# One-operand maxima and sums, a turned ring of banks, and two loads moved in SP's queue

## The chip, the cores and the metric

The kernel runs on one core of one Trainium2 chip. The time is that of one execution on the device, in microseconds, and the median over the runs counts. One further execution was profiled; its trace and its page are what the profile below is read from.

Engine names: PE is TensorE (PEld its weight loads), DVE is VectorE, ACT is ScalarE, POOL is GpSimd, SP is SyncE, which only issues DMAs here.

## What is computed

Two attentions over the same shapes, side by side in the output: sequence 2048, width 576, 32 heads of 18. A is a dilated sliding window of 8 keys, B is full attention.

```python
def _A_ref(x, wqkv, wo):
...
    W, dil = 8, 2
...
    q, k, v = qkv[0], qkv[1], qkv[2]
    off = jnp.arange(W) * dil
    idx = pos[:, None] - off[None, :]
...
    kg = k[:, :, idx_c, :].reshape(B, H, S, W, Dh)
    vg = v[:, :, idx_c, :].reshape(B, H, S, W, Dh)
    logits = jnp.einsum("bhsd,bhswd->bhsw", q, kg) * scale
    logits = jnp.where(mask[None, None, :, :], logits, -1e9)
    attn = _softmax(logits, axis=-1)
    o = jnp.einsum("bhsw,bhswd->bhsd", attn, vg)
    return (lambda x, *d: x.transpose(*d))(o, 0, 2, 1, 3).reshape(B, S, D) @ wo

def _B_ref(x, wqkv, wo):
...
    scores = jnp.einsum("bhqd,bhkd->bhqk", q, k) * scale
    p = _softmax(scores, axis=-1)
    o = jnp.einsum("bhqk,bhkd->bhqd", p, v)
    return (lambda x, *d: x.transpose(*d))(o, 0, 2, 1, 3).reshape(B, S, D) @ wo

return jnp.concatenate([a, b], axis=-1)
```

## The kernel before

**Two parts in time.** The first part projects: B's and A's queries, keys and values by matmuls over the width, in split precision (each operand as a high and a low half). The second part, which the change is about, is one loop over 512 **steps**. Step s works on one key tile kt = s % 16 of 128 keys, one block b of 512 queries (four blocks) and one group g of four heads (eight groups): s = 64 g + 16 b + kt.

**One step of B.** TensorE makes four score tiles (`score`, L271; one bank of PSUM each, 128 keys x 512 queries), ScalarE turns each into exponentials (L279), and one step later four matmuls (L744, eight rows in the profile) multiply them with the values into the accumulating bank `po`. The values carry a column of ones, so `po` also holds the softmax's denominators. In the same step TensorE makes raw scores again for the maxima of a block that comes later (L160), and VectorE reduces three banks of them to maxima `mx` (L168). A matmul here uses one half of the array's rows; matmuls on the two halves run side by side when they alternate.

**Banks.** Seven banks stand in two rings: `scores` (0 to 3) and `else` (4 to 6, the maxima). `bank(kind)` takes the bank at the front of the ring, which was used longest ago, and puts it at the end. A matmul into a bank waits until its last reader (ScalarE or VectorE) is done.

**Double steps.** A's output product is put into the loop by `together`: it takes two steps at once, keeps one bank of the `scores` ring aside for the product, and makes the eight scores in the three others. After it ScalarE copies the product out as `y` (L1280), and the bank is put back at the end of the ring. The steps in front of double steps stand in the table `MADE`, which the code compares with the step through `producing` and the agenda.

**First steps of a block.** When kt is 0, `po` of the block before must be copied out (`finish`): on ScalarE inside a double step if one follows, otherwise on VectorE at once. `ahead` marks first steps in which the half maximum (`parts_of_maximum`) comes behind the first score and not in front of it.

**A's softmax.** A's 2048 rows go in eight sets (`local(j)`), each in an agenda of times relative to `AT[j]`. POOL makes the logits `lg` (128 x 8 window places x 64), VectorE the maxima `am`, POOL subtracts them, ScalarE takes the exponentials in place, VectorE makes the sums `as` and their inverses, POOL multiplies. `over_window` (L937 to L943) folds the eight window places in three `tensor_tensor` instructions, of 256, 128 and 64 elements a partition.

**Denominators.** For each block `finish` loads the denominators out of the copied `po` through DMA (`den<-o`, L787), VectorE takes the reciprocal (L788), it is stored and read back spread out (`drec<-den` L789, `rec<-drec` L790), and POOL multiplies (L791). The agenda fixes at which step each of these is issued, so the reciprocal's place in VectorE's order is fixed.

**The last group.** For g = 7 the finished rows of the groups before, called old rows, are loaded back (`fetch_old(b)`, L1070) as the operand of B's output product: four chunks a block, two loads of 252 KB a chunk. Block 1's go into the keys' tile of a set that is no longer used (`ks`).

**What sets the order.** Nothing is rearranged: each engine runs its instructions in the order in which the code writes them (`manual_schedule`), and `agenda[step]` decides what is written behind which step. SP's queue is one such order; a DMA that waits holds back every later one on it.

Of the kernel before, what the change touches and what calls it, by code (L numbers as in the profile page):

```python
# [7 lines left out]
F32 = mybir.dt.float32  # L8
# [3 lines left out]
ALU = mybir.AluOpType  # L12
AX = mybir.AxisListType
# [7 lines left out]
W = 8  # L21
# [8 lines left out]
SUB = AB // 4  # L30
HALO = DIL * (W - 1)

STEPS = NB * NT
# [11 lines left out]
MADE = ((96, 101, 112, 128), (144, 160, 176, 192), (208, 212, 224, 240), (256, 266, 272, 288),  # L45
        (307, 320, 336, 352), (368, 376, 384, 400), (417, 432, 440, 448), (474, 476, 478, 480))
# [15 lines left out]
def two_attentions(ctx: ExitStack, tc, xa, wa, woa, xb, wb, wob, out):  # L62
# [5 lines left out]
    nc = tc.nc  # L68
# [10 lines left out]
    rings = {"all": list(range(7)), "scores": [0, 1, 2, 3], "else": [4, 5, 6]}  # L79
# [28 lines left out]
    step = 0  # L108
# [4 lines left out]
    def plan(start, pieces):  # L113
        for n, f in pieces:
            agenda[start + n].append(f)
# [267 lines left out]
    with (tc.tile_pool(name="x", bufs=1, side="right") as xp,  # L383
# [103 lines left out]
        if True:  # L487
# [47 lines left out]
            ahead = deque()  # L535
# [147 lines left out]
            for k in range(2, 14):  # L683
                n = 46 if k == 2 else 36 + 4 * k
# [34 lines left out]
            for c, b in order:  # L719
                n = min(128, 3 * D - 128 * c)  # L720
# [14 lines left out]
        step = 0  # L735
# [166 lines left out]
    def local(j):  # L902

        st = {}
# [29 lines left out]
                    for w in range(1, W):  # L934
                        nc.gpsimd.memset(lg[:32, w, : DIL * w], MASKED)

        def over_window(op, name, n):  # L937

            if n == 0:
                st[name] = work.tile([128, W // 2, SUB], F32, name=name, bufs=1)  # L940
            t, half = st[name], W >> n + 1
            src = t if n else st["lg"]
            nc.vector.tensor_tensor(t[:, :half], src[:, :half], src[:, half : 2 * half], op=op)  # L943

        def most(n):
            over_window(ALU.max, "am", n)
# [5 lines left out]
            nc.scalar.activation(st["lg"], st["lg"], AF.Exp, scale=SCALE)  # L952

        def total(n):
            over_window(ALU.add, "as", n)

        def inverses(n):
            half = st["as"][:, 0, SUB // 2 * n : SUB // 2 * n + SUB // 2]
            nc.vector.reciprocal(half, half)

        def share():
# [47 lines left out]
        def sums_of_a(h, n, alone=True):  # L1009
# [7 lines left out]
            if not alone:  # L1017
# [4 lines left out]


        soon = SOON[j]
        sums = ((36, 37, 38), (38, 39)) if j in (0, 2, 5) else ((36, 36, 37), (38, 39))
        late = soon % 3
        pieces = [(33, lower), (35, exponents), (39, share), (60 + late, upper), (61 + late, rest), (64 + late, lambda: put(0)), (66 + late, lambda: put(1))]

        pieces[:0] = [(at, lambda f=f, n=n: f(n)) for f, ats in ((most, (31, 32, 33)), (total, sums[0]),
                                                                (inverses, sums[1])) for n, at in enumerate(ats)]  # L1030
        for c in range(DH // 2):
            pieces.append((39 + 5 * c // 2 + late, lambda c=c: weighted(c)))
# [18 lines left out]
    def fetch_old(b, start=0, end=4):  # L1051
        for c in range(start, end):
            h, n = 7 * c, 126
            if b < 2:

                t = sets[(NG - 2) % 3][b]
                o = ap(t[:, c, 0] if b == 0 else t[:, c // 2, 1024 * (c % 2) :], (512, 2), (1, 512))
                o = o[:, 0], o[:, 1]

            elif b == 2:  # L1060
                o = [work.tile([128, D], F32R, name=nm, bufs=5)[:, :512] for nm in ("wohi", "wolo")]
            elif c < 2:
                o = work.tile([128, 2, 512], F32R, name="pr", bufs=2)
                o = o[:, 0], o[:, 1]
            else:
                o = ap(work.tile([128, DH, HALO + SUB], F32R, name="akv", bufs=2), (512, 2), (1, 512))
                o = o[:, 0], o[:, 1]
            for i in range(2):
                first = do[i, h // 4, 32 * (h % 4), 512 * b : 512 * b + 512]
                load(o[i].bitcast(F32)[:n], rows(first, (32 * S, 7), (S, DH), (1, 512)))  # L1070
            olds[b].append([t[:n] for t in o])
# [24 lines left out]
    sums = {}  # L1096
# [125 lines left out]
    for g in range(1, NG):  # L1222
        if g > EARLY:
            plan(STEPS * (g - 2) + 1, [(n, f) for n, f in enumerate(stack_loads(g))])
        if g == NG - 1:
            plan(STEPS * g, [(4, lambda: fetch_old(0)), (6, lambda: fetch_old(1, 0, 2)), (12, lambda: fetch_old(1, 2, 4)),
                             (34, lambda: fetch_old(3)),
                             (38, lambda: fetch_old(2))])
            plan(STEPS * g, [(n, lambda t=t, h=h: partial(t, h)) for n, (t, h) in
                             zip((43, 44, 45, 47, 49, 51), [(t, h) for t in range(3) for h in range(2)])])  # L1230
            plan(STEPS * g, [(62, lambda: outside.append(lambda: first(3, NB - 1, 0)))])
            for b in range(NB - 1):
                producing.update(STEPS * g + NT * (b + 1) + (23, 15, 7)[b] + n for n in range(8))
        plan(STEPS * (g - 1), [(24, lambda g=g: load_v(g))])
# [7 lines left out]
    def together(both, y):  # L1242

        at = [(*divmod(s // NT, NB), s % NT) for s in (step, step + 1)]
        es = [[None] * 4 for _ in range(2)]
        ps = bank("scores")[:, : y.shape[1]]
        held = rings["scores"].pop()
        exps = deque()

        def one(i, h):  # L1250
            f = score(*at[i], h, put_off=True)
            exps.append(lambda: es[i].__setitem__(h, f()))

        def others(r):
            return [f for i in range(2) for h in (r, r + 2)
                    for f in (lambda i=i, h=h: one(i, h), lambda: maximum(r)())[:: 1 - 2 * r]]

        def piece(r, k):
            a, b = both[r][k]
            return nc.tensor.matmul(ps, a, b, start=r == k == 0, stop=r == 1 and k == len(both[1]) - 1)  # L1260

        def in_turn(*lanes):

            for _, f in sorted(((at + every * k, f) for fs, at, every in lanes for k, f in enumerate(fs)), key=lambda p: p[0]):
                f()
                while len(exps) > 1:
                    exps.popleft()()

        last = []
        in_turn(([lambda k=k: last.append(piece(0, k)) for k in range(len(both[0]))], 0, 133), (others(1), 1, 235))  # L1270
        between = nc.scalar.nop()
        sync(between, last[-1])
        upper = others(0)
        if leaving:
            upper[2] = lambda f=upper[2], copy=leaving.pop(): (f(), exps.popleft()(), copy())
        in_turn(([lambda k=k: sync(piece(1, k), between) if k == 0 else piece(1, k) for k in range(len(both[1]))], 240, 133),
                (upper, 0, 235))
        while exps:
            exps.popleft()()
        nc.scalar.activation(y, ps, AF.Copy)  # L1280
        rings["scores"].append(held)
        return [(*at[i], es[i]) for i in range(2)]

    paired = False
# [2 lines left out]
    while step < ALL:  # L1287
        n, kt = divmod(step, NT)
        g, b = divmod(n, NB)
        es = [None] * 4  # L1290

        if inside and inside[0] in for_two and kt and len(ready) == 1 and total - sum(given) >= 8 and step + 4 < ALL:
            new = together(*inside.pop(0)(False))
            assert not leaving
            due()
            step += 1
            weigh(*ready, new[0])
            ready[:] = new[1:]
            due()
            step += 1  # L1300
            continue

        while leaving:
            leaving.pop()()

        whole = total - sum(given) > 1
        parts = (bool(begun) or total - sum(given) > 3) and step not in copied

        ps = bank() if inside and whole else None


        ahead = kt == 0 and (n < 6 or n >= 24)
        part = [parts_of_maximum()] if parts and not ahead else []
        for h in (0, 2, 1, 3):

            if inside and h == 3:
                inside.pop(0)()
            es[h] = score(g, b, kt, h, between=(lambda: part.append(parts_of_maximum())) if parts and ahead and h == 0 else None)
            if h == 0 and whole:
                maximum(1, ps)()  # L1320
            if h == 1 and parts:
                part[0]()
            if h == 3 and whole:
                maximum(0)()
        if sum(given) == total and not begun:
            settle()
        for fs in (behind_scores, outside):
            while fs:
                fs.pop(0)()

        paired = paired or kt % 2 == 0 and sum(given) == total and not begun
        for _ in range(1 if paired and step < ALL - 2 else len(waiting)):
            if waiting:
                waiting.pop(0)()
        if ready and (kt % 2 == 0 or not paired):
            weigh(ready.pop(0))
        ready.append((g, b, kt, es))
        if paired and kt % 2:
            weigh(*ready)
            ready.clear()  # L1340
        due()

        if len(waiting) > (0 if not paired else 2 if kt % 2 else len(waiting)):
            waiting.pop(0)()
        step += 1
# [24 lines left out]
```

## Time and profile before

| what | value |
|---|---|
| median of three runs | 1601.35 us (1600.4 to 1601.88) |
| profiled execution | 1600.95 us, its span 1599.2 us |
| chain, by line | po L744 29%, bank L271 18%, bank L160 17%, bank L366 14%, mx L168 3%, den<-o 1% |
| ACT L279 (exponentials) | 2048 of 606 ns on average |
| DVE L168 (maxima) | 2048 of 683 ns on average |
| DVE idle in front of L788 | 3.3 us, ended by DMA den<-o |

The span runs from the first to the last instruction; the execution's time is a little longer than the span. TensorE is busy nearly throughout, but its ends are modelled, so a matmul that waited reads as a longer one. What a stretch costs is read from the distances between the starts of the same group of matmuls, one group a step. A row of a timeline has start, duration, engine, line, operation and tiles, and in brackets the idle time in front of it with what ended it. A row of busy time by stretch has, for PE, PEld, DVE, ACT and POOL, the busy microseconds and the count, then the granted clock of TensorE (1.00 is full), the DMA engines' share, and GB/s.

### The profile page before, as it was taken

Reading aid. Unit: us, or ns where it says so; the run is one execution under the profiler, and the core shown is the slowest. Engines: PE = TensorE matmul, PEld = TensorE weight load, DVE = VectorE, ACT = ScalarE, POOL = GpSimd, SP = SyncE. Lnnn points to the kernel's source line nnn. Section 1 sums busy time; section 2 is a strip of 40 time slices with the busy share of each in tenths; the row PEclk is TensorE's granted clock in tenths of the full one; section 3 lists DMA queues with packets and bytes.
Section 4 is the critical chain, followed back from the end, with each engine's and each line's share of the span. In section 5 each row is a group of like instructions: output and inputs, shape, how many; then the busy total and the mean of one; then the engine's idle time right before and its main releaser. Section 6 shows DMA issues by size and latency. Waiting matters only on the chain.

```text
span 1599.2 us, 34971 instructions
## 1 busy us (share of the span) xinstructions
PE 1583.9 (99%) x13276; PEld 966.4 (60%) x13276; DVE 1365.8 (85%) x2315; ACT 1214.7 (76%) x2438; POOL 965.4 (60%) x798
## 2 busy tenths in 40 slices
PE   9999999999999999999999999999999999999998
PEld 7999889999543445444545444445445445545676
DVE  5299999999999999999999999999999999997522
ACT  6423441121699999999999999999999999997655
POOL 2405742211166995896897896897897799771000
PEclk9999999999999999999999999999999999999999
DMA  8937954532312362245225324422721331154311
GB/s 239 242 126 202 270 163 128 159 102 70 74 34 70 73 143 65 69 121 107 74 80 132 82 87 120 107 78 54 142 94 43 90 100 50 46 182 123 129 62 61
DMA packets 188025, 175.66 MB, mean 110 GB/s; under 512 B 119416, under 2 KB 133240, under 8 KB 186128
## 3 DMA queue, kind: packets, MB, share of 16 engines
q1 hardware_dynamic: 182992, 161.88, 36.7%
q0 software_dynamic: 4032, 10.63, 3.3%
q8 instruction: 104, 1.70, 0.5%
q10 hardware_dynamic: 832, 0.92, 0.2%
q14 instruction: 65, 0.53, 0.1%
HBM read 98.77 MB, written 73.47 MB: 108 GB/s over the span
## 4 chain that ended last, share of the span: by engine, by line
PE 90%; DVE 4%; DMA 3%; ACT 2%; POOL 1%; issue 0%; POOLq 0%; DVEq 0%; SPq 0%
PE po L744 29%; PE bank L271 18%; PE bank L160 17%; PE bank L366 14%; PE bank L303 5%; PE bank L1133 4%; PE bank L1260 4%; DVE mx L168 3%; DMA dqk<-olo 1%; DMA den<-o 1%; ACT e L279 1%; POOL xlo L414 1%; DMA dqk<-ohi 1%; DMA first<-wb 0%; DVE am L943 0%
## 5 line engine op out<-in xcount | busy, mean ns | idle before, releaser
L168 DVE TENSOR_REDUCE mx<-bank 128x2 f32<-128x512 f32 x2048 | 1279.4, 683 | 122.3 <-PE bank L160 91.2
L279 ACT ACTIVATE e<-bank 128x512 f32<-128x512 f32 x2048 | 1047.0, 606 | 66.5 <-PE bank L271 59.6
L160 PE MATMUL bank<-ks,qs 54*128 54x512 f32 (+1 forms) x2466 | 790.1, 381 | 7.1 <-DVE mx L168 5.6
L160 PEld LDWEIGHTS bank<-ks,qs 54*128 54x128 f32 x2466 | 404.0, 184 | 390.4 <-DVE mx L168 342.8
L271 PE MATMUL bank<-qs,ks 56*128 56x512 f32 x2048 | 595.0, 425 | 0.1
L744 PE MATMUL po<-e,v 128*19 128x512 f32 x4096 | 532.2, 599 | 0.0
L271 PEld LDWEIGHTS bank<-qs,ks 56*128 56x128 f32 x2048 | 309.1, 185 | 29.3 <-ACT e L279 22.5
L925 POOL TENSOR_TENSOR pr<-aq,akv 128x1024 f32<-128x1024 f32 x72 | 158.5, 2203 | 15.8 <-DMA akv<-da 13.0
L968 POOL TENSOR_TENSOR pr<-lg,akv 128x1024 f32<-128x1024 f32 x72 | 158.2, 2198 | 0.5
L744 PEld LDWEIGHTS po<-e,v 128*19 128x19 f32 x4096 | 73.8, 97 | 138.5 <-issue 133.0
L929 POOL TENSOR_TENSOR pr<-pr 128x1024 f32<-128x1024 f32 x64 | 152.6, 2385 | 5.0
L694 ACT ACTIVATE ohi<-bank 128x512 f32<-128x512 f32 (+1 forms) x56 | 30.4, 595 | 149.5 <-issue 122.6
L366 PE MATMUL bank<-xhi,ahi 64*128 64x512 f32 (+1 forms) x448 | 115.1, 387 | 0.0
L366 PE MATMUL bank<-xhi,alo 64*128 64x512 f32 (+1 forms) x448 | 111.4, 387 | 0.0
L366 PE MATMUL bank<-xlo,ahi 64*128 64x512 f32 (+1 forms) x448 | 108.9, 388 | 0.1
L1260 PE MATMUL bank<-wohi,at 64*128 64x288 f32 x480 | 103.3, 304 | 0.0
L969 POOL TENSOR_TENSOR pr<-pr 128x512 f32<-128x512 f32 x72 | 92.5, 1284 | 5.6
L1260 PEld LDWEIGHTS bank<-wohi,at 64*128 64x128 f32 x480 | 74.7, 184 | 27.5 <-ACT e L279 23.8
L414 POOL TENSOR_TENSOR alo<-raw,ahi 128x512 fp32r<-128x512 f32 (+1 forms) x14 | 17.6, 1255 | 121.3 <-ACT ahi L413 78.5
L506 POOL TENSOR_TENSOR olo<-olo,ohi 128x512 fp32r<-128x512 f32 x36 | 46.2, 1296 | 66.8 <-ACT ohi L505 59.4
L1260 PE MATMUL bank<-wolo,at 64*128 64x288 f32 x240 | 69.9, 291 | 0.0
L366 PEld LDWEIGHTS bank<-xhi,ahi 64*128 64x128 f32 (+1 forms) x448 | 65.0, 181 | 2.7
(202 smaller groups left out, 1793.8 us busy)
## 6 DMA issues: line engine op xcount, KB each, us to landing
do<-n SPq DMA_DIRECT2D x30, 512.0 KB
da<-ohi SPq DMA_DIRECT2D x52, 256.0 KB
akv<-da SPq DMA_DIRECT2D x64, 175.5 KB
out<-y SPq DMA_DIRECT2D x32, 288.0 KB
qs<-dqk SPq DMA_DIRECT2D x30, 288.0 KB
ks<-dqk SPq DMA_DIRECT2D x30, 288.0 KB
at<-dao SPq DMA_DIRECT2D x60, 128.0 KB
rec<-drec SPq DMA_DIRECT2D x29, 256.0 KB
```

What stands on the lines that cost most here:

```text
L160: return nc.tensor.matmul(ps if part is None else ps[:, 256 * r : 256 * r + 256], qs[at, b, p, 128 * t : 128 * t + 128], ks[at, p, 512 * k ...
L168: nc.vector.tensor_reduce(at, ps.rearrange("q (s n) -> q s n", s=2), axis=AX.X, op=ALU.max)
L271: nc.tensor.matmul(ps, ks[at, p, 128 * kt : 128 * kt + 128], qs[at, b, p], start=True, stop=True)
L279: nc.scalar.activation(e, ps, AF.Exp, scale=SCALE)
L303: nc.tensor.matmul(ps, a, b, start=c == i == 0, stop=c == 4 and i == 1)
L366: nc.tensor.matmul(ps, a, b, start=start, stop=stop)
L744: nc.tensor.matmul(po[32 * i : 32 * i + 19], vs[g][:, kt, 19 * i : 19 * i + 19], es[i], start=kt == 0, stop=kt == NT - 1)
L925: nc.gpsimd.tensor_mul(pr, ap(st["q"][:, 2 * c], (SUB, 2), (0, W), (1, SUB)), window(st["k"], c))
L929: nc.gpsimd.tensor_add(st["pr"], st["pr"], pr)
L968: nc.gpsimd.tensor_mul(at, ap(st["lg"], (0, 2), (SUB, W), (1, SUB)), window(st["v"], c))
L969: nc.gpsimd.tensor_add(at[:, :, :4], at[:, :, :4], at[:, :, 4:])
L1260: return nc.tensor.matmul(ps, a, b, start=r == k == 0, stop=r == 1 and k == len(both[1]) - 1)
```

## The change

Four edits:

- `over_window` uses `tensor_reduce` on the logits alone, seen with the window places innermost (a step of 64 elements), a half of the 64 columns at a time. The maxima take two instructions (at 32 and 33, in place of 31, 32 and 33); the sums take two in sets 0, 2 and 5 and one in the others. 48 instructions become 27.
- At the end of `together` the ring of score banks is turned by one more.
- `ahead` is off in first steps that stand in `MADE`. With the table as it is these are the steps 384, 400, 432 and 448.
- The second half of block 1's old rows is fetched at step 472 in place of 460.

```diff
-        def over_window(op, name, n):
+        def over_window(op, name, n, parts=2):
             if n == 0:
-                st[name] = work.tile([128, W // 2, SUB], F32, name=name, bufs=1)
-            t, half = st[name], W >> n + 1
-            src = t if n else st["lg"]
-            nc.vector.tensor_tensor(t[:, :half], src[:, :half], src[:, half : 2 * half], op=op)
+                st[name] = work.tile([128, SUB], F32, name=name, bufs=1)
+            some = SUB // parts
+            cols = slice(some * n, some * n + some)
+            nc.vector.tensor_reduce(st[name][:, cols], st["lg"][:, :, cols].rearrange("p w n -> p n w"), axis=AX.X, op=op)
...
         def total(n):
-            over_window(ALU.add, "as", n)
+            over_window(ALU.add, "as", n, len(sums[0]))
...
-            half = st["as"][:, 0, SUB // 2 * n : SUB // 2 * n + SUB // 2]
+            half = st["as"][:, SUB // 2 * n : SUB // 2 * n + SUB // 2]
...
-        sums = ((36, 37, 38), (38, 39)) if j in (0, 2, 5) else ((36, 36, 37), (38, 39))
+        sums = ((36, 37) if j in (0, 2, 5) else (36,), (38, 39))
...
-        pieces[:0] = [(at, lambda f=f, n=n: f(n)) for f, ats in ((most, (31, 32, 33)), (total, sums[0]),
+        pieces[:0] = [(at, lambda f=f, n=n: f(n)) for f, ats in ((most, (32, 33)), (total, sums[0]),
...
-            plan(STEPS * g, [(4, lambda: fetch_old(0)), (6, lambda: fetch_old(1, 0, 2)), (12, lambda: fetch_old(1, 2, 4)),
+            plan(STEPS * g, [(4, lambda: fetch_old(0)), (6, lambda: fetch_old(1, 0, 2)), (24, lambda: fetch_old(1, 2, 4)),
...
         rings["scores"].append(held)
+        rings["scores"].append(rings["scores"].pop(0))
...
-        ahead = kt == 0 and (n < 6 or n >= 24)
+        ahead = kt == 0 and (n < 6 or n >= 24) and step not in sum(MADE, ())
```

SP's queue around the moved loads, from the store of a finished block (`do<-n`) to the next read of spread reciprocals (`rec<-drec`). `den<-o` are the denominators of block 0 of the last group, `dao` A's stored rows, `at`, `ahl` and `aq` their loads. Before:

```order
L789 DMA drec<-den 128x16
L1070 DMA ks_88<-do 126x1x512 x4
L858 DMA y<-wob 126x576
L983 DMA dao<-aohi 128x1152
L790 DMA rec<-drec 128x1x512
L983 DMA dao<-ao 128x1152
L787 DMA den<-o 128x1x16
```

The end of the same queue's piece now, from the last loads of A's rows on; the rows of the fence above stand as they were, without the four loads:

```order
L998 DMA aq<-dao 128x4x64 x2
L1000 DMA aq<-dao 64x2x64
L789 DMA drec<-den 128x16
L1070 DMA ks_88<-do 126x1x512 x4
L779 DMA do<-n 128x2x512
L790 DMA rec<-drec 128x1x512
L197 DMA qs_1531<-mh 2x8x32 x4
```

The four loads moved behind `den<-o`, all loads of A's rows and the next `drec<-den`, and in front of `do<-n`, `rec<-drec` and the loads of the next block's maxima (`qs<-mh`).

VectorE's order at the maxima of the fifth set (j = 4), before:

```order
L168 TENSOR_REDUCE mx<-bank_15608 128x2
L943 TENSOR_TENSOR am<-lg 128x256
L168 TENSOR_REDUCE mx<-bank_15625 128x2
L168 TENSOR_REDUCE mx<-bank_15618 128x2
L168 TENSOR_REDUCE mx<-bank_15642 128x2
L943 TENSOR_TENSOR am<-am 128x128
L168 TENSOR_REDUCE mx<-bank_15658 128x2
L168 TENSOR_REDUCE mx<-bank_15651 128x2
L168 TENSOR_REDUCE mx<-bank_15675 128x2
L943 TENSOR_TENSOR am<-am 128x64
```

and now:

```order
L168 TENSOR_REDUCE mx<-bank_15630 128x2
L943 TENSOR_REDUCE am<-lg 128x32
L168 TENSOR_REDUCE mx<-bank_15647 128x2
L168 TENSOR_REDUCE mx<-bank_15640 128x2
L168 TENSOR_REDUCE mx<-bank_15664 128x2
L943 TENSOR_REDUCE am<-lg 128x32
```

The first of the three places, one step earlier, is gone; at each of the two others stands a reduction from `lg`. The shape shown is that of the output: 32 maxima of eight elements each.

TensorE's order in step 384, the first of a block, behind the value products of the step before. Before:

```order
L744 MATMUL po<-e,v 19x512 x4
L271 MATMUL bank_20115<-qs_87,ks_88 128x512
L160 MATMUL bank_20117<-ks_88,qs_87 128x256
L160 MATMUL bank_20122<-ks_88,qs_87 128x512
L271 MATMUL bank_20125<-qs_87,ks_88 128x512
```

and now:

```order
L744 MATMUL po<-e,v 19x512 x4
L160 MATMUL bank_20097<-ks_88,qs_87 128x256
L271 MATMUL bank_20100<-qs_87,ks_88 128x512
L160 MATMUL bank_20104<-ks_88,qs_87 128x512
L271 MATMUL bank_20107<-qs_87,ks_88 128x512
```

The half maximum (L160, 256 columns) moved in front of the first score (L271), so that scores and maxima alternate from the start. The order of the other engines is as it was, but for the numbers of the score banks.

## The prediction

> **What bounds the kernel now.** First the page (busy shares, the chain that ended last), then the pace of TensorE in an undisturbed stretch of the attention loop, then every place where that pace breaks.
>
> ```profile
> span 1599.2 us, 34971 instructions
> PE 1583.9 (99%) x13276; PEld 966.4 (60%) x13276; DVE 1365.8 (85%) x2315; ACT 1214.7 (76%) x2438; POOL 965.4 (60%) x798
> PE 90%; DVE 4%; DMA 3%; ACT 2%; POOL 1%; issue 0%; POOLq 0%; DVEq 0%; SPq 0%
> 1058.12:1098.93 40.81, 19.84 (x156) 2.68 (x160) 1.00 0.30 71
> ```
>
> TensorE sets the end: 90% of the chain. The last row counts the weight loads of the values' line (L744), eight to a step: 160 in 40.81 us are 20 steps of 2.04 us. A single step is the distance between two starts of the L744 group, so anything above 2.04 is lost time, also where the modelled ends call the engine busy. VectorE is the close second: it takes three maxima a step. The 4% of DVE and part of the 3% of DMA in the chain are what this change can reach. The largest break in the whole loop is here (views: the timelines of PE and DVE, then busy time by stretch):
>
> ```profile
> 1439.35 1.06 PE L744 MATMUL po<-e,v 128*19 128x512 f32 x8
> 1441.40 1.05 PE L744 MATMUL po<-e,v 128*19 128x512 f32 x8
> 1446.96 1.91 PE L744 MATMUL po<-e,v 128*19 128x512 f32 x8
> 1450.18 1.05 PE L744 MATMUL po<-e,v 128*19 128x512 f32 x8
> ...
> 1438.96 1.89 DVE L168 TENSOR_REDUCE mx<-bank 128x2 f32<-128x512 f32 x3 [0.16 <-PE bank L160]
> 1444.16 0.25 DVE L788 RECIPROCAL den<-den 128x16 f32<-128x16 f32 x1 [3.31 <-DMA den<-o]
> ...
> 1446.30:1449.00 2.70, 2.70 (x15) 0.58 (x15) 1.84 (x3) 1.91 (x4) 0.00 (x0) 0.50 0.63 144
> ```
>
> The steps there are 2.05, 5.56 and 3.22 us. VectorE ended its maxima at 1440.85 and stood in front of the reciprocal of the denominators until their load landed near 1444.1; the maxima queued behind it held their banks, so TensorE stopped. The second long step is the stop's echo: the granted clock is 0.50 for 2.7 us after it. Over 2.04 the two cost 3.52 + 1.18 = **4.70 us**.
>
> **The moved loads (two chunks of old rows, step 460 to 472).** The queue of SP in order, with the size of one load, the rate of the stretch, and who reads what stands behind the new place:
>
> ```profile
> 1425.68 0.76 SPq L789 DMA_DIRECT2D drec<-den  x1
> 1426.48 3.35 SPq L1070 DMA_DIRECT2D ks<-do  x4
> 1429.87 0.70 SPq L858 DMA_DIRECT2D y<-wob  x1
> ...
> 1432.38 0.59 SPq L787 DMA_DIRECT2D den<-o  x1
> ...
> 1450.85 0.56 SPq L790 DMA_DIRECT2D rec<-drec  x1
> ...
> ks<-do SPq DMA_DIRECT2D x8, 252.0 KB
> ...
> 1432.40:1444.10 11.70, 10.05 (x80) 4.15 (x78) 7.86 (x13) 10.54 (x21) 3.35 (x3) 1.00 0.65 220
> ...
> 1458.86 0.21 POOL L103 CAST mh<-mt 128x32 fp32r<-128x32 f32 x1 [12.76 <-DVE mt L185]
> 1459.36 1.29 POOL L791 TENSOR_TENSOR o<-o,rec 128x512 f32<-128x512 f32 x1
> ```
>
> Four loads of 252 KB (1008 KB) took SP 3.39 us from 1426.48 to the next issue, and their bytes lay in front of the 8 KB of denominators, which needed 11.7 us to land. Without them the denominators are issued up to 3.39 us earlier; I count 2.7, since the issue of rec in between must first see drec land. And 1008 KB at 220 GB/s are 4.6 us less to move. The landing therefore falls between 1441.4 (earlier issue alone, same latency) and 1436.8 (both in full). VectorE wants it at 1440.85. So the worst bound leaves about 0.6 us of the stop, the best none. I take no stop, with some two microseconds in hand, and the clock then does not fall: **-4.7 us**, bounds -4.1 and -4.7.
>
> What the same four loads cost at the new place: they stand behind drec and in front of do, rec and the eight short loads of the next block's maxima. SP now issues rec 6.8 us after the landing (1444.1 to 1450.85); with a landing near 1438 and the four issues in between (3.39 us) that becomes 1448.2. Its reader is POOL's multiply, which now starts right behind the split of the maxima at 1459.36, after POOL idled 12.76 us for VectorE; with the stop gone that is near 1454.7. So 6.5 us of room are left where 8.5 were, and the 1008 KB need 4.6 of them. I price it at nothing, covered by POOL's idling; without that cover it is up to 4.6 us. The old rows themselves are read by the sums of block 1, which the code plans at step 494 and later.
>
> **Maxima and sums in one-operand form.** Eight sets; 48 two-operand VectorE instructions become 27 reductions: 16 for the maxima, 11 for the sums, of 256 elements each but for five of 512.
>
> ```profile
> L943 DVE TENSOR_TENSOR am<-am x16: 206/246/446, 500.5 to 1354.7; 128x128 f32<-128x128 f32 x8, 128x64 f32<-128x64 f32 x8
> L943 DVE TENSOR_TENSOR am<-lg x8: 413/416/1462, 497.9 to 1350.2; 128x256 f32<-128x256 f32 x8
> L943 DVE TENSOR_TENSOR as<-lg x8: 415/424/493, 508.9 to 1362.4; 128x256 f32<-128x256 f32 x8
> L178 DVE TENSOR_REDUCE m<-mx x32: 273/276/286, 125.6 to 1503.7; 128x16 f32<-128x128 f32 x32
> L168 DVE TENSOR_REDUCE mx<-bank 128x2 f32<-128x512 f32 x2048 | 1279.4, 683 | 122.3 <-PE bank L160 91.2
> ...
> 746.06 0.41 DVE L943 TENSOR_TENSOR am<-lg 128x256 f32<-128x256 f32 x1
> 746.39 0.24 DVE L788 RECIPROCAL den<-den 128x16 f32<-128x16 f32 x1
> ...
> 985.04 1.46 DVE L943 TENSOR_TENSOR am<-lg 128x256 f32<-128x256 f32 x1
> 984.93 1.29 POOL L793 TENSOR_TENSOR n<-o,n 128x512 fp32r<-128x512 f32 x1
> ...
> 498.51 1.05 PE L744 MATMUL po<-e,v 128*19 128x512 f32 x8
> 501.04 1.05 PE L744 MATMUL po<-e,v 128*19 128x512 f32 x8
> 503.19 1.05 PE L744 MATMUL po<-e,v 128*19 128x512 f32 x8
> ...
> 985.67 1.05 PE L744 MATMUL po<-e,v 128*19 128x512 f32 x8
> 988.79 1.05 PE L744 MATMUL po<-e,v 128*19 128x512 f32 x8
> ...
> 1228.01 1.05 PE L744 MATMUL po<-e,v 128*19 128x512 f32 x8
> 1230.18 1.05 PE L744 MATMUL po<-e,v 128*19 128x512 f32 x8
> ```
>
> A reduction of 128 elements takes 276 ns and of 512 takes 683 ns, so about 1.06 ns an element: 412 ns for 256, the same as the old first fold (416). The next instruction starts 0.33 us after such a start (746.06 to 746.39). An old set held VectorE 0.33 + 0.20 + 0.20 = 0.73 us, a new one 0.66, or 0.60 as one piece. Undisturbed, that is next to nothing. The gain is in the disturbed ones: the fold of 1462 ns began under a POOL instruction on two SBUF operands and ended only after it, at 985.04, while the 32 reductions from SBUF in L178 spread by 13 ns in all although POOL is busy 60% of the time. TensorE lost 1.08 us there (985.67 to 988.79) and 0.60 in the first set (498.51 to 503.19). Against that, each new 0.33 us piece in a plain step can cost what one such fold costs undisturbed, 0.13 us (1228.01 to 1230.18), and eight of the sixteen maxima pieces fall in plain steps, outside double steps: up to 1.0. Four old folds of that size cost about 0.5 there already. Balance of the maxima 1.08 + 0.60 + 0.5 - 1.0 = 1.2; the shorter sums, mostly hidden in the wake of double steps, 0.1: **-1.3 us**. Bounds: -2.3 if the pieces hide wholly; +3.0 if reading with a step of 64 elements doubles the element time (22 pieces longer by 0.27 us and five by 0.53, 8.6 us, half of it hidden, on top of the -1.3).
>
> A rule speaks for that last end: the Trainium skill, "SBUF — State Buffer", section "Door 1: The DMA port swizzle", says that an access to SBUF pays once it leaves a 16-byte line, so beyond a step of four fp32 values. By it each element of these reductions would pay, and at twice the element time the whole sum would be -2.2 us; no row here shows a VectorE reduction with such a step.
>
> **The two small edits.** Four first steps of a block (384, 400, 432, 448) start with the half maximum again instead of a score. Step 384:
>
> ```profile
> 1248.49 1.05 PE L744 MATMUL po<-e,v 128*19 128x512 f32 x8
> 1250.65 1.05 PE L744 MATMUL po<-e,v 128*19 128x512 f32 x8
> ...
> 832.89 0.47 ACT L1280 ACTIVATE y<-bank 128x288 f32<-128x288 f32 x1
> 833.77 0.50 PE L271 MATMUL bank<-qs,ks 56*128 56x512 f32 x1
> ```
>
> It takes 2.16 us, 0.12 over the pace, where the two halves of the array are out of turn; no copy of po runs on VectorE in these four. **-0.5 us**, bounds 0 and -0.6. Turning the ring of score banks makes the first score behind a double step take the bank of the seventh exponential, and the third that of y. In this double step y is read by 833.36 and the first score starts at 833.77: every bank is long free behind the sixteen value products. **0**, and up to 0.1 us a double step if a semaphore comes later.
>
> **The sum.** -4.7 - 1.3 - 0.5 = -6.5 on the profiled execution's 1600.95 us (span plus 1.75 around it): 1594.45. The median of the runs is 0.4 above it: **1594.8**.
>
> **The rivals.** (a) The denominators still land late, behind the other loads and A's stores, which stay in front of them in SP's queue (1429.87 to 1432.38). For it: 11.7 us of latency is more than twice what 1008 KB explain. Against it: both bounds above. Two microseconds late leave some 2.5 of the 4.7: about 1597.3. (b) Strided reductions are slow: +3.0 in place of -1.3, 1599.1. For it: each element lies 256 bytes behind the last. Against it: nothing in these rows. (c) Slower than before: the moved loads push rec and the eight short loads of the next block's maxima (SP issues them right behind rec), and TensorE's first score of block 1 waits. It decides once rec lands later than 6.5 us after its issue; if the full 3.39 us of issue and 4.6 us of transfer come out there and the clock falls again (1.18), 9.2 us are lost against 6.5 gained: 1604. Against it: issue and transfer overlap, and the moved loads are issued before rec. (d) The turned ring also frees the second step behind double steps, some 0.08 us in each of thirty: 1592.4.
>
> **How the numbers follow.** Forecast 0.70, (a) 0.10, (b) 0.08, (c) 0.07, (d) 0.05. The forecast's own span is 1593 to 1596.3. The range 1592.8 to 1597.8 takes in (a) and leaves out (b), (c) and half of (d), 0.18. A run of this kernel tells 0.2% (3.2 us) from no change: faster means below 1598.1, which holds for the forecast, (a) and (d), and for a milder (b), a quarter of it: 0.87; within 0.2%: the rest of (b) and a mild (c), 0.07; slower: 0.06.
>
> **What would show it.** Right: no idle time of VectorE in front of the last L788; steps near 2.04 and granted clock 1.00 from 1440 to 1450; L943 in 27 records with maxima near their medians of 0.4 and 0.7 us; the four first steps at 2.04. Wrong: records of L943 near 0.7 us for 256 elements; a new idle stretch of TensorE between 1450 and 1490; a value product group late behind double steps.

## The result, and the profile after

| | before | the change |
|---|---|---|
| median, first comparison (7 and 7 runs) | 1601.35 us (1598.12 to 1603.9) | 1596.23 us (1594.88 to 1598.06) |
| ratio | | 0.997, 95% interval 0.9959 to 0.9982 |
| profiled execution | 1600.95 us, span 1599.2 | 1597.76 us, span 1596.0 |
| first to last L744 group (the loop) | 1166.49 us | 1162.52 us |

The change is 5.1 us faster between the medians, where 6.5 was forecast. The profiled execution of the change is one of its slower runs: the projections ahead of the loop, which the change doesn't touch, took 1.2 us more in it: the granted clock stood at 0.50 there from 175.42 to 178.84 us, and at 1.00 throughout that part in the execution of before. So the parts are compared inside the loop, where 3.97 us went.

From the page of the change, its size, TensorE's line and the chain by engine:

```profile
span 1596.0 us, 34951 instructions
PE 1583.2 (99%) x13276; PEld 969.1 (61%) x13276; DVE 1367.7 (86%) x2294; ACT 1216.6 (76%) x2438; POOL 964.6 (60%) x798
PE 92%; DVE 5%; DMA 1%; ACT 1%; POOL 1%; issue 0%; SPq 0%; POOLq 0%; DVEq 0%; ACTq 0%
```

VectorE has 21 instructions fewer and is busy 1.9 us longer. The DMA share of the chain fell from 3% to 1%, VectorE's rose from 4% to 5%: one wait is gone, and the new instructions are longer than the ones they replaced.

The stretch of the old stop, in the timelines of PE and DVE and in busy time by stretch (the granted clock is the 1.00 behind POOL's 0.00):

```profile
1441.19 1.05 PE L744 MATMUL po<-e,v 128*19 128x512 f32 x8
1443.23 1.05 PE L744 MATMUL po<-e,v 128*19 128x512 f32 x8
1445.26 1.05 PE L744 MATMUL po<-e,v 128*19 128x512 f32 x8
...
1442.60 0.24 DVE L788 RECIPROCAL den<-den 128x16 f32<-128x16 f32 x1
...
1446.30:1449.00 2.70, 2.70 (x26) 1.46 (x24) 2.40 (x5) 2.70 (x7) 0.00 (x0) 1.00 0.36 113
```

The distances are 2.04 and 2.03 where they were 5.56 and 3.22, no idle time stands in front of L788, and the clock doesn't fall. SP's queue in the change, then POOL's timeline:

```profile
1427.01 0.75 SPq L789 DMA_DIRECT2D drec<-den  x1
...
1430.91 0.58 SPq L790 DMA_DIRECT2D rec<-drec  x1
...
1432.11 0.60 SPq L787 DMA_DIRECT2D den<-o  x1
...
1449.12 0.61 SPq L790 DMA_DIRECT2D rec<-drec  x1
...
1459.67 1.30 POOL L791 TENSOR_TENSOR o<-o,rec 128x512 f32<-128x512 f32 x1 [3.15 <-DMA rec<-drec]
```

The denominators are issued 5.10 us behind the store of drec, 6.70 before: 1.6 us gained of the 2.7 that I counted, since rec still waits for drec to land. The rest is latency. The last packet of the 8 KB ends 6.8 us after the issue, at 1438.9 (11.1 us before), and VectorE wants it at 1442.60, 3.7 us later; before, 0.6 us passed between the last packet and the reciprocal, so some 3 us are in hand. Behind the new place POOL now waits 3.15 us for rec. TensorE doesn't notice: from 1447 to the end of the loop its distances add up to those of before within 0.1 us.

The new instructions, by line (minimum, median and maximum in ns, first and last start):

```profile
L943 DVE TENSOR_REDUCE am<-lg x16: 596/603/624, 501.1 to 1356.2; 128x32 f32<-128x256 f32 x16
L943 DVE TENSOR_REDUCE as<-lg x11: 593/606/1073, 509.9 to 1364.3; 128x32 f32<-128x256 f32 x6, 128x64 f32<-128x512 f32 x5
```

A piece of 256 elements takes 0.60 us, not the 0.41 of the forecast. What that does in front of a double step (timelines of PE and DVE, the change):

```profile
1109.87 1.05 PE L744 MATMUL po<-e,v 128*19 128x512 f32 x8
1115.66 0.63 PE L744 MATMUL po<-e,v 128*19 128x512 f32 x4
...
1111.55 0.61 DVE L943 TENSOR_REDUCE am<-lg 128x32 f32<-128x256 f32 x1
1112.08 4.26 DVE L168 TENSOR_REDUCE mx<-bank 128x2 f32<-128x512 f32 x7
```

The double step takes 5.79 us. In the same place before it took 5.18, with a fold of 0.22 us in front of the seven maxima.

All distances between L744 groups, sorted by what the change did at the place (before to after, us in the loop):

| place | difference |
|---|---|
| the stop near 1441 (5.56 + 3.22 to 2.03 + 2.04) | -4.7 |
| steps with maxima and sums of A | +2.1 |
| first steps 384, 400, 432, 448 (2.17, 2.16, 2.17, 2.16 to 2.02, 2.37, 2.64, 2.37) | +0.7 |
| second steps behind double steps (2.12 to 2.06, 26 of them: -1.7; one of 2.40 to 2.06) | -2.0 |
| together | -3.9 |

### The profile page after: what moved, and what is told of

Read it like the earlier page. It is cut to its first block, busy times and chain, and to the rows that moved or that the text cites. A ratio compares the mean times of both kernels' runs of the same rounds, so it can differ in the third digit from the quotient of the medians.

```text
span 1596.0 us, 34951 instructions
## 1 busy us (share of the span) xinstructions
PE 1583.2 (99%) x13276; PEld 969.1 (61%) x13276; DVE 1367.7 (86%) x2294; ACT 1216.6 (76%) x2438; POOL 964.6 (60%) x798
## 4 chain that ended last, share of the span: by engine, by line
PE 92%; DVE 5%; DMA 1%; ACT 1%; POOL 1%; issue 0%; SPq 0%; POOLq 0%; DVEq 0%; ACTq 0%
PE po L744 29%; PE bank L271 18%; PE bank L160 17%; PE bank L366 15%; PE bank L303 5%; PE bank L1260 4%; PE bank L1133 4%; DVE mx L168 4%; POOL xlo L414 1%; ACT e L279 0%; DMA dqk<-olo 0%; DVE am L943 0%; DMA first<-xb 0%; DMA more<-xa 0%; DMA dqk<-ohi 0%
## 5 line engine op out<-in xcount | busy, mean ns | idle before, releaser
L160 PE MATMUL bank<-ks,qs 54*128 54x512 f32 (+1 forms) x2466 | 789.0, 381 | 4.2 <-DVE mx L168 3.4
L160 PEld LDWEIGHTS bank<-ks,qs 54*128 54x128 f32 x2466 | 404.1, 184 | 390.2 <-DVE mx L168 343.8
L271 PE MATMUL bank<-qs,ks 56*128 56x512 f32 x2048 | 592.2, 425 | 0.1
L744 PE MATMUL po<-e,v 128*19 128x512 f32 x4096 | 531.3, 598 | 0.0
L271 PEld LDWEIGHTS bank<-qs,ks 56*128 56x128 f32 x2048 | 308.3, 184 | 25.5 <-ACT e L279 18.8
L744 PEld LDWEIGHTS po<-e,v 128*19 128x19 f32 x4096 | 73.8, 97 | 138.2 <-issue 132.8
```

The lines of the kernel that those rows point to most:

```text
L160: return nc.tensor.matmul(ps if part is None else ps[:, 256 * r : 256 * r + 256], qs[at, b, p, 128 * t : 128 * t + 128], ks[at, p, 512 * k ...
L271: nc.tensor.matmul(ps, ks[at, p, 128 * kt : 128 * kt + 128], qs[at, b, p], start=True, stop=True)
L744: nc.tensor.matmul(po[32 * i : 32 * i + 19], vs[g][:, kt, 19 * i : 19 * i + 19], es[i], start=kt == 0, stop=kt == NT - 1)
```

## The experiments

Each kernel was profiled, and its L744 distances were compared with those of before. Where an expectation gives a step's number that isn't a first step of a block, it counts the distances between L744 groups from 0, which is two less than the code's step. The groups of runs on one chip share the runs of before: median 1601.34 for the first four, 1600.76 for the next four, 1601.5 for the last. Runs of before alone spread from 1597 to 1604 us, so where a kernel ran once its time decides nothing; the distances of its profiled execution do.

**The moved loads alone.**

```diff
-(12, lambda: fetch_old(1, 2, 4))
+(24, lambda: fetch_old(1, 2, 4))
```

> The kernel before with the moved loads alone. Theory (the stop in front of the reciprocal of the denominators is the whole effect): the steps of 5.56 and 3.22 us become 2.04 each, the loop is 4.7 us shorter, the granted clock stays 1.00 from 1440 to 1450, every other step is as before. Rival (the loads collide again behind their new place): a new long step between 1445 and 1490, and the loop gains less than 3 us.

Measured: 1597.75 us (10 runs), ratio 0.998, 95% interval 0.997 to 0.999; the loop 3.8 us shorter. The stop is gone (-4.7), no long step came in its place, and POOL waits 2.24 us for rec without harm. About 0.8 us went at another place, a fold of set 3's sum that took 0.58 us in the profiled execution of before. Timelines of POOL, DVE and PE of this kernel:

```profile
879.88 1.31 POOL L791 TENSOR_TENSOR o<-o,rec 128x512 f32<-128x512 f32 x1 [5.81 <-DMA rec<-drec]
880.08 1.26 DVE L943 TENSOR_TENSOR as<-as 128x128 f32<-128x128 f32 x1
881.00 1.05 PE L744 MATMUL po<-e,v 128*19 128x512 f32 x8
...
883.62 1.05 PE L744 MATMUL po<-e,v 128*19 128x512 f32 x8
```

A two-operand fold of 128 elements, 0.25 us elsewhere, lasts 1.26: it began beneath a POOL instruction on two SBUF operands and ended only after it, and the step takes 2.62. POOL's start here hangs on a DMA, so whether they meet differs between executions: they also met in the kernels of the turn alone and of the first steps alone, whose folds at that place are the same. The edits of the moved loads and of the first steps come only later in the loop, so up to here these kernels do what before does.

**The turn of the ring alone.**

```diff
         rings["scores"].append(held)
+        rings["scores"].append(rings["scores"].pop(0))
```

> The kernel before with the turned ring of score banks alone. Theory (the first exponential behind a double step waits for two semaphores, and the turn gives that to the fourth, which stands in a queue anyway): the second step behind a double step falls from 2.12 to 2.05 us in each of some 28 places, the loop is about 1.8 us shorter, and the first exponential there starts 0.53 us after its score where it was 0.60. Rival (as predicted, the turn does nothing): those steps stay at 2.12, 0 us.

Measured: 1599.06 us (one run). The second steps behind double steps come to a median of 2.056 (2.12 before), but for one of 2.63 where set 3's sum met POOL as above, and the one of 2.40 comes to 2.06. Without the 2.63 that is -2.0 together, the same as in the whole change. The whole loop is 1.9 us shorter: a stop that was 0.9 shorter and folds that lasted longer (+0.9) cancel. So rival (d) holds. Why is seen in one double step, timelines and instructions by line, first before:

```profile
1257.68 0.49 PE L271 MATMUL bank<-qs,ks 56*128 56x512 f32 x1
...
L279 ACTq EVENT_SEMAPHORE  x1: 17/17/17, 1258.2 to 1258.2; - x1
...
1258.27 1.57 ACT L279 ACTIVATE e<-bank 128x512 f32<-128x512 f32 x3 [0.98 <-PE bank L271]
...
1258.70 1.05 PE L744 MATMUL po<-e,v 128*19 128x512 f32 x8
1260.83 1.05 PE L744 MATMUL po<-e,v 128*19 128x512 f32 x8
```

and the same place in the change (the run of the turn alone has the same order there):

```profile
1259.30 0.50 PE L271 MATMUL bank<-qs,ks 56*128 56x512 f32 x1
...
1259.83 1.57 ACT L279 ACTIVATE e<-bank 128x512 f32<-128x512 f32 x3 [0.92 <-PE bank L271]
...
1260.32 1.05 PE L744 MATMUL po<-e,v 128*19 128x512 f32 x8
1262.38 1.05 PE L744 MATMUL po<-e,v 128*19 128x512 f32 x8
...
L279 ACTq EVENT_SEMAPHORE  x1: 17/17/17, 1260.4 to 1260.4; - x1
```

A semaphore is the signal by which one engine tells another that it is done. A separate semaphore wait is an instruction of its own in a queue, for a second signal that the instruction behind it needs. Before, the first exponential behind the double step has such a wait in front of it and starts 0.59 us after its score; without one it starts after 0.53. ScalarE is idle there (0.98 us), so the 0.06 passes on to everything behind: the step takes 2.13 and not 2.06. In the change the wait stands at 1260.4, in front of the third exponential (not of the fourth, as I had expected), where ScalarE has work queued. The wait itself lasts 17 ns, so it was already met; it cost all the same. In the one step of 2.40 the same wait stands in front, but the exponential starts 0.88 us after its score, and 0.54 with the turn; why it is so much there, 0.3 of the 2.0, no run shows.

**The one-operand maxima and sums alone.** The edit is that of `over_window`, its times and its readers, as shown in the change.

> The kernel before with the one-operand maxima and sums alone. Theory (reading with a step of 64 elements costs 1.8 ns an element): records of 600 ns for 256 elements and 1065 ns for 512, the step of 3.12 us gone, and the loop 2 us longer (1.5 to 2.6). Rival (as predicted, the freedom from POOL outweighs it): the loop 1.3 us shorter.

Measured: 1599.37 us (one run), the loop 1.0 us shorter. Its stop was 3.70 + 2.05 and thus 3.0 us shorter than in the profiled execution of before, with the loads where they were:

```profile
1444.43 0.25 DVE L788 RECIPROCAL den<-den 128x16 f32<-128x16 f32 x1 [1.77 <-DMA den<-o]
```

Less the stop's 3.0, the reductions cost 2.0 us, as in the change. The largest gain is in the step of set 4, 3.12 to 2.02, where the old fold lasted 1.46; in set 0 2.53 falls to 2.04, and four more steps with old folds gain 0.10 to 0.18. Together the maxima gain 2.1 us in these six steps and lose 3.7 in others, 2.2 of it in six double steps (0.29 to 0.62 each).

**The first steps alone.**

```diff
-        ahead = kt == 0 and (n < 6 or n >= 24)
+        ahead = kt == 0 and (n < 6 or n >= 24) and step not in sum(MADE, ())
```

> The kernel before with the order of the four first steps alone. Theory (in steps 400, 432 and 448 TensorE's queue clears the semaphores of the block's maxima loads in front of the first score; with the half maximum first that is no longer hidden): step 384 0.14 us shorter, the three others 0.2 us longer each, the loop 0.5 us longer. Rival (as predicted): each of the four 0.12 us shorter, the loop 0.5 us shorter.

Measured: 1601.17 us (one run). Step 384 falls from 2.17 to 2.04; 400, 432 and 448 rise from 2.16 to 2.35, 2.54 and 2.36: +0.6 together. The rest of the loop's +0.3 is a stop 1.0 us shorter and the meeting of set 3's sum with POOL, 0.8. Step 400, PE's timeline and L271 by line, in the change:

```profile
1284.99 1.05 PE L744 MATMUL po<-e,v 128*19 128x512 f32 x8
1285.98 0.38 PE L160 MATMUL bank<-ks,qs 54*128 54x256 f32 x1
1286.37 0.47 PE L271 MATMUL bank<-qs,ks 56*128 56x512 f32 x1
...
1287.36 0.63 PE L744 MATMUL po<-e,v 128*19 128x512 f32 x4
...
L271 PEldq EVENT_SEMAPHORE  x4: 51/51/51, 1285.9 to 1286.3; - x4
```

and L271 in the same step before, then in step 384 of the change:

```profile
L271 PEldq EVENT_SEMAPHORE  x4: 51/51/51, 1283.1 to 1283.4; - x4
```

```profile
L271 PEldq EVENT_SEMAPHORE  x1: 51/51/51, 1251.2 to 1251.2; - x1
```

The first score of a block has four separate semaphore waits (for the loads of the block's maxima, `qs`). With the score in front they were over before the value products began at 1283.45. With the half maximum in front of it they come beneath that half maximum, and the score starts 0.39 us after it instead of beside it. Step 384 has one such wait, its score starts 0.06 us after the half maximum, and it gains. That the waits are the cause is read from these rows; no run takes them away by themselves.

**Sums that read neighbours.** The change, but the sums of sets 1 to 7 read eight elements that lie side by side (other elements than the reference sums), so that only the step between elements differs.

```diff
-            nc.vector.tensor_reduce(st[name][:, cols], st["lg"][:, :, cols].rearrange("p w n -> p n w"), axis=AX.X, op=op)
+            src = st["lg"][:, :, cols].rearrange("p w n -> p n w")
+            if op == ALU.add and j:
+                src = ap(st["lg"][:, W * some * n // SUB], (W, some), (1, W))
+            nc.vector.tensor_reduce(st[name][:, cols], src, axis=AX.X, op=op)
```

> The changed kernel, but the sums of sets 1 to 7 read eight neighbouring elements for each result in place of eight with a step of 64 (so these sums are over other elements; set 0 and all maxima as in the change). Theory (the step costs the time): these sums take 0.41 us for 256 elements and 0.68 us for 512, while the maxima beside them stay at 0.60. Rival (a reduction from SBUF to many short groups is slow at any step): they stay at 0.60 and 1.06 us.

Measured: 1596.85 us (one run). Its reductions, by line:

```profile
L946 DVE TENSOR_REDUCE as<-lg x11: 408/604/687, 509.9 to 1363.8; 128x32 f32<-128x256 f32 x6, 128x64 f32<-128x512 f32 x5
...
L946 DVE TENSOR_REDUCE am<-lg x16: 595/604/612, 501.0 to 1355.7; 128x32 f32<-128x256 f32 x16
```

Four pieces of 256 took 0.41 us, the two of set 0, which still read with the step, 0.60; those of 512 took 0.69 us in place of 1.06. The maxima stayed at 0.60. The loop is 1.04 us shorter than that of the change itself on the same chip (its second profile, below), and 0.92 of it lies in four steps at the sums of sets 2, 5 and 7. The step between elements is the cause, and in the sums alone it costs about 1 us.

**The ring turned by two.**

```diff
         rings["scores"].append(held)
+        for _ in range(2):
+            rings["scores"].append(rings["scores"].pop(0))
```

> The kernel before with the ring of score banks turned by two behind double steps. Theory (the exponential with two waits must not be the first): it is then the third, and the second step behind a double step takes 2.05 us as with one turn; loop some 1.8 us shorter. Rival (what helps is that the first score takes the bank of the seventh exponential): with the bank of the eighth in front the step is not 2.05 but 2.12 or longer.

Measured: 1598.3 us (one run). Second steps of 2.05 to 2.07, but for one of 2.71 where a fold lasted 1.19 us. The loop is 2.2 us shorter, 0.9 of it at the stop. Turned by one or by two, the separate wait leaves the first exponential for the third, and the gain behind double steps is the same; so it isn't the bank of the seventh exponential that helps.

**The parts that pay, put together.** The moved loads and the turn as in the change; `ahead` off at step 384 alone; the sums of sets 1, 3, 4 and 6, whose reductions cost TensorE nothing in the change, in one operand; all maxima and the other sums in two operands as before, with the maxima of set 4 later.

```diff
-        ahead = kt == 0 and (n < 6 or n >= 24)
+        ahead = kt == 0 and (n < 6 or n > 24)
...
-        sums = ((36, 37, 38), (38, 39)) if j in (0, 2, 5) else ((36, 36, 37), (38, 39))
+        sums = ((36, 37, 38), (38, 39)) if j in (0, 2, 5) else ((36,), (38, 39)) if j != 7 else ((36, 36, 37), (38, 39))
...
-(most, (31, 32, 33))
+(most, (32, 33, 33) if j == 4 else (31, 32, 33))
```

> The kernel before with the moved loads, the turned ring, the other order in step 384 alone, one-operand sums only where VectorE waits behind a double step (sets 1, 3, 4, 6), and the two-operand maxima of set 4 one step later. Theory: against the change, the loop loses the 2 us that strided reductions cost in plain steps and the 0.2 us in each of steps 400, 432 and 448: the loop is 2.0 to 2.8 us shorter than the change's, near 1160. Rival (two-operand folds collide with POOL at new places, as the first maximum of set 4 did): the step of 3.12 us comes back at another place and nothing is gained on the change.

Measured: 1593.96 us (1593.2 to 1595.38, 5 runs), ratio 0.9959, 95% interval 0.9945 to 0.9972; the loop 6.5 us shorter than before and 2.7 shorter than the change's. Every run is below every run of the change on the same chip. The rival's collision came as well: set 4's step fell from 3.12 to 2.03, but a fold of set 6 met POOL (timelines of POOL, DVE and PE):

```profile
1224.55 1.29 POOL L793 TENSOR_TENSOR n<-o,n 128x512 fp32r<-128x512 f32 x1
1224.90 1.23 DVE L943 TENSOR_TENSOR am<-lg 128x256 f32<-128x256 f32 x1
1225.53 1.05 PE L744 MATMUL po<-e,v 128*19 128x512 f32 x8
...
1228.51 1.05 PE L744 MATMUL po<-e,v 128*19 128x512 f32 x8
```

That step takes 2.98 us.

**The change again**, beside the last three on one chip.

> The changed kernel once more, beside the one above on the same chip. Theory: as in its first profile, maxima at 0.60 us, second steps behind double steps at 2.05, first steps 400, 432 and 448 near 2.37 or more, no stop near 1441; some 5 us faster than before.

Measured: 1596.55 us (1595.76 to 1597.56, 11 runs), before 1600.76; ratio 0.9973, 95% interval 0.9965 to 0.9982. The loop is 3.79 us shorter than before, place by place as in the first profile.

**The maxima of sets 0 and 6 later too.**

```diff
-(most, (32, 33, 33) if j == 4 else (31, 32, 33))
+(most, (32, 33, 33) if j in (0, 4, 6) else (31, 32, 33))
```

> The version of the last but one run with one more edit: the two-operand maxima of sets 0 and 6 are also issued at 32, 33 and 33, as those of set 4 are. Theory (a two-operand fold costs when its reads fall under a GpSimd instruction on two SBUF operands, so the place decides): step 373, 2.98 us in that version, comes back to 2.05-2.2, the two long steps of set 0 (2.57 and 2.16) lose about 0.3 together, the loop is 1.0-1.3 us shorter, near 1158.8, the time near 1592.8. Rival (the shift of everything behind by half a microsecond moves another fold under a GpSimd instruction): 373 is mended and as much is lost elsewhere, the loop stays within 0.4 of 1160.

Measured: 1595.01 us (1593.21 to 1595.68, 5 runs), ratio 0.9961, 95% interval 0.9946 to 0.9975; the loop 1160.01 us, 1159.96 in the last but one. The fold of set 6 (DVE and PE):

```profile
1227.26 1.05 PE L744 MATMUL po<-e,v 128*19 128x512 f32 x8
1228.63 0.41 DVE L943 TENSOR_TENSOR am<-lg 128x256 f32<-128x256 f32 x1
1229.27 1.05 PE L744 MATMUL po<-e,v 128*19 128x512 f32 x8
```

The place does decide: 0.41 us, and a step of 2.01. But the double step behind it took 0.22 more, set 0 took 0.11 more instead of 0.3 less, a fold of set 7 took 0.14 less, and some 0.8 us are spread over the whole loop in pieces of at most 0.05. The loop went as the rival said; the two versions can't be told apart.

## Why the prediction was right, and where it wasn't

The forecast's sign and the time were near, 1594.8 against 1596.2, but three of its four terms had the wrong size, two of them the wrong sign. In the loop they were off by +3.4, +1.2 and -2.0 us; two rivals with small chances both came true and in part offset each other. So it was in part luck that the time came out so near.

- **The moved loads, -4.7: right**, in the whole change and alone. The way was another one: issue gained 1.6 us and not 2.7, the latency did the rest. The term was read from one execution. In five profiled executions with the loads at their old place (before, and the kernels of the turn, the reductions, the first steps and the turn by two, which differ in other places) the two long steps exceed 2 x 2.04 by 4.7, 3.8, 1.7, 3.7 and 3.8 us, 3.5 on average. So the profile of before was at the upper end, and the gain over many runs is probably smaller than the forecast's: the moved loads alone took 3.6 between medians. The 1.7 belongs to the stop of the reductions alone, behind which the clock didn't fall. Busy time by stretch, two stretches of before and two of that kernel:

```profile
1442.79:1446.20 3.41, 0.59 (x6) 0.52 (x7) 1.99 (x4) 0.21 (x2) 3.14 (x3) 1.00 0.47 105
1446.20:1449.61 3.41, 3.41 (x18) 1.29 (x17) 1.89 (x3) 2.01 (x4) 0.00 (x0) 0.50 0.70 160
...
1444.40:1447.81 3.41, 1.93 (x16) 0.84 (x16) 3.26 (x7) 1.75 (x4) 1.88 (x2) 1.00 0.59 134
1447.81:1451.23 3.42, 3.42 (x32) 1.74 (x32) 3.11 (x7) 3.42 (x8) 0.00 (x0) 1.00 0.66 156
```

  The clock stood at 0.50 for 3.41 us, not for the 2.7 of the stretch that the prediction looked at. In the eleven traces it changes only on a grid of 3.41 us, and (but for the first and last 10 us) a stretch of that grid was at 0.50 when TensorE had been idle, by its modelled ends, for 1.70 us or more of the stretch before, seven times, and at 1.00 when it had been idle for 1.63 us or less. By this the length of a stop and its place on the grid decide whether it has an echo. It is read from the traces; no kernel was made to test it.
- **The cost behind them, 0: right, though its cover was thinner.** I left 6.5 us between rec's issue and its use; POOL got it 10.5 us after the issue, 3.15 late. That was the point from which rival (c) was to decide. It didn't, because TensorE needs nothing of POOL's soon after: the wait ends on POOL.
- **The one-operand form, -1.3: wrong, +2.1.** The failing step is "412 ns for 256, the same as the old first fold". That price came from reductions of neighbouring elements; with a step of 64 elements a piece takes 0.60 us and holds VectorE for 0.53 (1111.55 to 1112.08) instead of 0.33. A second step failed with it: the sum charged only the eight maxima pieces outside double steps, up to 1.0 us, and took those in double steps as free. With the reductions alone the maxima cost 3.7 us, of which 2.2 fall in six double steps. Rival (b), priced at +3.0 with a chance of 0.08, was the right mechanism. The gain from disturbed folds was right: 1.08 + 0.60 + 0.5 were forecast, and 2.1 came, 1.1 of it in set 4's step; no reduction stretched. The Trainium skill, "SBUF — State Buffer", section "Who interferes with whom", says that on trn2 a `tensor_reduce` never contends with GpSimd, while an instruction with two SBUF inputs does. The trace agrees: the 16 maxima of the change took 596 to 624 ns, and the two of them that began beneath a POOL instruction on two SBUF operands 606 and 614, while folds took up to 1.46 us. The rule on 16-byte lines in its section "Door 1: The DMA port swizzle", weighed in the prediction, agrees with the trace as well: 603 ns for 256 elements and up to 1073 for 512, where neighbours take 0.41 and 0.69 us. Only a step of 256 bytes was run, so from which step on it costs no run here shows.
- **The first steps, -0.5: wrong, +0.7** (+0.6 alone; step 432 also holds a piece of set 7's maxima). Step 384, from which the price was taken, does gain 0.14. The failing step is its use for all four: the other three have four semaphore waits in front of the first score, and by the rows above the swap exposes them.
- **The turned ring, 0: wrong, -2.0.** That "every bank is long free" is not the point: a wait that is already met still costs its 0.06 us where the engine behind it is idle. I had its size as rival (d) at 2.4 us, with a chance of 0.05, but not this reason.

What stays open: how much of the 3.7 us that the maxima's pieces cost is the step between elements and how much their new places, since no kernel ran with maxima that read neighbours (for the sums the runs show 1.0 for the step); whether the four waits alone make the swap lose; and how long the stop of before is in the runs that weren't profiled.

## What to carry to other kernels

Price an instruction from rows with the same step between elements as well as the same count, and a swap from every place at which it happens, counting the separate semaphore waits in front of the instruction there. In these traces a wait that was long met was free only where its engine had work queued; move it to an instruction that stands behind others. Before a stop in one profile is entered at its full size, look for what in it hangs on a DMA, because it will differ from run to run.

## What the runs showed that I had not expected

- A reduction on VectorE over elements 256 bytes apart goes on at 1.8 ns an element (from 604 ns for 256 to 1064 for 512, means), over neighbours at 1.08 (from 409 to 686). The forecast had the second, and twice that as a rival; I had no row for the first.
- One separate semaphore wait in front of an exponential costs 0.06 us (0.59 against 0.53 us after the score); four in front of a score held it back by 0.39 us, in steps that grew by 0.2 to 0.4.
- 8 KB that a DMA brings behind other loads landed 10.9 to 12.0 us after the issue with 1008 KB more issued in front of it (five profiles), and 6.2 to 6.9 without (six).
- TensorE's granted clock halved for 3.41 us after a stretch of 3.41 us in which TensorE had been idle for half of the time (1.70 us in the projections of the change).
- A two-operand fold of 128 elements, 0.25 us, lasts 1.26 beneath a POOL instruction on two SBUF operands, and whether the two meet can change from one execution to the next.
